# ScalarE's reads behind the latest written exponential, two buffers for the key halves, and a decoder in place, in the attention stage of a fused attention and feed-forward kernel

## The chip, the cores and the metric

One core of a Trainium2 chip runs the whole program. Its engines are TensorE (PE, and PEld for its weight loads), VectorE (DVE), ScalarE (ACT), GpSimd (POOL) and SyncE (SP, which issues nearly all DMAs). The metric is the device time of one execution in microseconds; the median of several executions is compared.

## The reference

Three layers follow each other. Shapes: q, k, v are 8 x 8 x 576 x 64 (batch, head, position, width), so there are 4608 tokens of 512 features after the attention.

```python
def _attn_ref(q, k, v):
    scores = scale * np.matmul(q, k.transpose(0, 1, 3, 2))
    mask = block_i >= block_j              # blocks of 64 positions
    scores = np.where(mask, scores, -1000000000.0)
    attn = np.exp(scores - np.max(scores, axis=-1, keepdims=True))
    attn = attn / (np.sum(attn, axis=-1, keepdims=True) + 1e-09)
    return np.matmul(attn, v)
...
def _moe_ref(x, phi, w1, w2):              # 8 experts of 4 slots
    logits = x @ phi
    d = softmax of logits over the tokens;  slot_input = d.T @ x
    slot_out[e] = np.maximum(slot_input[e] @ w1[e], 0.0) @ w2[e]
    c = softmax of logits over the slots;   return c @ slot_out
...
def _moe2_ref(x, w_in, w_out):
    h = np.maximum(x @ w_in, 0.0)
    return h * h @ w_out
```

The two matrices of the last layer, w_in (512 x 2048) and w_out, arrive as 64-bit floats; the kernel turns them into 32-bit floats itself, which it calls decoding.

## The kernel before, in words

**Stages.** The attention comes first and fills the span up to about 430 us; the logits and the token softmax of the expert layer run inside it, one batch behind. Then come the experts, then the feed-forward layer.

**The attention's loop.** Two heads make a pair; there are 32 pairs, four per batch (`j` is the pair's number in its batch, `b` the batch). `pair(n)` writes in one go: the scores and exponentials of pair `n` (`scores`, seven chunks: six of 128 x 512 at line 552 and a small one, `pd`, at line 534), the maxima of pair `n + 2` (`maxpass`, seven chunks, reduced by VectorE at line 451), the product with v of pair `n - 1` (`pv`), and the preparation of pair `n + 3` (`split`). `split` has ScalarE write a 16-bit high half of q (`high_q`) and of k (`high`, line 401, into the tile `ka`), VectorE the low half next to it (`low`, line 405), and SP transposes `ka` into `s1` by DMA (line 412). The q half is turned on TensorE and copied out by ScalarE (line 425).

**Slots.** The code of a pair is laid out over eight slots. In slot `i` stand chunk `i` of the scores with its exponential, and chunk `i` of the maxima. Slot 0 also has the two last chunks of the maxima, `split`, and nearly all of `pv`. After a slot's chunks up to four loads are taken from the queue `dq`, then one step from `aux`, or if that is empty (and not in slot 0) one from `decq`, and in some slots one step from `work` (the expert layer's softmax of the batch before).

- `aux` gets, in each odd pair from the third to the 27th, `scale` for the pairs `n + 4` and `n + 5`: four squares with a running sum on ScalarE (`square`, line 342, output `junk`, one each for k and q of two pairs), then `chain`, which begins with the TensorE matmul `ps_ssq` (line 349) and goes on with eight small VectorE steps to the scales `sig` and `es`. So the squares stand in slots 0 to 3 and `ps_ssq` in slot 4. Pairs 1 and 2 hold the same for pairs 4 to 6.
- `decq` gets the steps of one w_in chunk: `flush` on ScalarE (line 168), then `keep`, `shift`, `sign`, `low` on VectorE (lines 172 to 190). There are 16 chunks of 512 KB; each is loaded by `load_in` (line 894) into one of two `raw` buffers.
- `dq` gets, in pair `n`, the loads of q and k of pair `n + 7` (lines 316, 323) and of v of pair `n + 2` (lines 294, 300), a w_in chunk when one is due, and some chunks of the experts' weights (lines 152, 154).

**Order.** The whole loop stands under

```python
        with tc.manual_schedule(engines={mybir.EngineType.PE}):
            for n in range(N + 1):
                pair(n)
```

so TensorE runs its instructions as the code writes them. On the other engines the compiler's scheduler chooses the order when the program is built: by readiness in its own model of the time, then by the place in the code. On the chip each engine then runs its list in that order, and an instruction whose operand isn't there holds all that come after it on that engine. Semaphores between the engines are put in by the compiler.

**Buffers.** PSUM: six banks `ps_r` are shared by scores, maxima and small products, and two more take `pv`. SBUF: `ka` and `qa` have one buffer each in the pool `nat` (pairs 1 and 3 borrow others); the decoder has one `dec_sq` and one `dec_hf` of 2 KB per partition in the pool `dec`; q and k of one batch lie in one of two arenas, `ar_lo` and `ar_hi`.

Of the kernel before, what the change touches and what calls it, by code (L numbers as in the profile page):

```python
# [8 lines left out]
F32 = mybir.dt.float32  # L9
F32R = mybir.dt.float32r  # L10
F16 = mybir.dt.float16
U32 = mybir.dt.uint32
# [11 lines left out]
def tile_attn_soft_moe_ffn(  # L24
# [43 lines left out]
    lg = const.tile([128, NTILE, NSL], F32, name="lg")  # L68
    acc = const.tile([128, DM], F32, name="acc")
    tot = const.tile([128, 1], F32, name="tot")  # L70
    so = const.tile([128, KD, NSL], F32, name="so")
    mrun = [const.tile([128, 1], F32, name=f"mrun{i}") for i in range(2)]

    lo_p = ctx.enter_context(tc.tile_pool(name="low", bufs=1, side="right"))
# [28 lines left out]

    wots = {}
    w_st = ExitStack()

    def qk_tile(b):
        t = (ar_lo, ar_hi[:, 9 * 512:18 * 512])[b % 2].rearrange("p (w x j d) -> p w x j d", w=2, j=NJ, d=D)
        return dict(q=t[:, 0], k=t[:, 1])
# [52 lines left out]
    def decode(pool, dst, raw, w):  # L162
        hi, lo = raw[:, :, 1], raw[:, :, 0]
        t = {}

        def flush():
            t["sq"] = pool.tile([128, w], F32, tag="dec_sq", name="dec_sq")
            nc.scalar.activation(out=t["sq"], in_=hi.bitcast(F32), func=AF.Square)

        def keep():  # L170
            t["hf"] = pool.tile([128, w], F32, tag="dec_hf", name="dec_hf")
            nc.vector.scalar_tensor_tensor(
                out=t["hf"], in0=t["sq"], scalar=2.0 ** -30, in1=hi.bitcast(F32), op0=ALU.is_ge, op1=ALU.mult
            )

        def shift():
            t["b"] = t["sq"].bitcast(U32)
            nc.vector.tensor_scalar(
                out=t["b"], in0=t["hf"].bitcast(U32), scalar1=3, scalar2=0x3FFFFFF8,
                op0=ALU.logical_shift_left, op1=ALU.bitwise_and,  # L180
            )

        def sign():
            nc.vector.scalar_tensor_tensor(
                out=t["b"], in0=t["hf"].bitcast(U32), scalar=0xC0000000, in1=t["b"],
                op0=ALU.bitwise_and, op1=ALU.bitwise_or,
            )

        def low():
            nc.vector.scalar_tensor_tensor(  # L190
                out=dst.bitcast(U32), in0=lo, scalar=29, in1=t["b"], op0=ALU.logical_shift_right, op1=ALU.bitwise_or
            )

        return [flush, keep, shift, sign, low]
# [29 lines left out]
    def attention():  # L224
# [111 lines left out]
        def scale(ns):  # L336
            w = len(ns)
            small = lambda nm, k=2, bufs=2: sm_p.tile([128, k, 2], F32, tag=nm, name=nm, bufs=bufs)[:, :, 0:w]
            ssq = sm_p.tile([128, 2, w], F32, tag=f"ssq{w}", name="ssq")

            def square(i, nm, c):
                nc.scalar.activation(
                    out=junk, in_=qk_tile(ns[c] // NJ)[nm][:, :, ns[c] % NJ, :], func=AF.Square, accum_out=ssq[:, i, c:c + 1],
                    saturate=False,
                )

            def chain():
                ps = ps_r.tile([128, 512], F32, tag="r", name="ps_ssq")
                nc.tensor.matmul(ps[:, 0:2 * w], ones[:, 0:1].to_broadcast([128, 128]), ssq.rearrange("p a c -> p (a c)"), start=True, stop=True)
                a, hb, g, inv = [small(nm) for nm in ("sc_a", "sc_h", "sc_g", "inv")]  # L350
                sig, es = small("sig", bufs=4), small("es", 1, 4)
                nc.vector.tensor_scalar(
                    out=a, in0=ps[:, 0:2 * w].rearrange("p (a c) -> p a c", a=2), scalar1=1e-30, scalar2=None, op0=ALU.max
                )
                nc.vector.tensor_scalar(
                    out=hb.bitcast(U32), in0=a.bitcast(U32), scalar1=1, scalar2=0x7F800000,
                    op0=ALU.logical_shift_right, op1=ALU.bitwise_and,
                )
                nc.vector.tensor_scalar(
                    out=g.bitcast(U32), in0=hb.bitcast(U32), scalar1=0x7F800000, scalar2=None,  # L360
                    op0=ALU.bitwise_xor,
                )
                nc.vector.tensor_scalar(out=sig, in0=g, scalar1=2.0 ** -51, scalar2=None, op0=ALU.mult)
                nc.vector.tensor_scalar(out=inv, in0=hb, scalar1=2.0 ** 50, scalar2=None, op0=ALU.mult)
                nc.vector.scalar_tensor_tensor(
                    out=sig[:, 1], in0=inv[:, 0], scalar=2.0 ** 20, in1=sig[:, 1], op0=ALU.mult, op1=ALU.min
                )
                nc.vector.scalar_tensor_tensor(
                    out=inv[:, 1], in0=sig[:, 0], scalar=2.0 ** -20, in1=inv[:, 1], op0=ALU.mult, op1=ALU.max
                )  # L370
                nc.vector.scalar_tensor_tensor(
                    out=es[:, 0], in0=inv[:, 0], scalar=1.0 / float(D) ** 0.5, in1=inv[:, 1],
                    op0=ALU.mult, op1=ALU.mult,
                )
                for c, n in enumerate(ns):
                    sc[n] = (sig[:, :, c], es[:, 0, c:c + 1])

            return [lambda i=i, nm=nm, c=c: square(i, nm, c) for c in range(w) for i, nm in ((1, "k"), (0, "q"))] + [chain]
# [3 lines left out]
        def split(n):  # L382
            b, j = divmod(n, NJ)
            if n in (1, 3):
                qa, ka = [
                    xT_p.tile([128, S], F32, tag="xt", name=nm).bitcast(F16).rearrange("p (s a d) -> p s a d", a=2, d=D)
                    for nm in ("qa", "ka")
                ]
                qa = qa[:, :, 0, :]
            else:  # L390
                qa = nat_p.tile([128, NBLK, D], F16, tag="qa", name="qa")
                ka = nat_p.tile([128, NBLK, 2, D], F16, tag="ka", name="ka")
            tr = (tr_a, tr_a, even, odd)[j]
            t1 = tr.tile([128, NBLK, 128], F16, tag="t1", name="t1")
            s1 = tr.tile([128, NBLK, 128], F16, tag="s1", name="s1")
            qbn, s2n = qb[n % NBQ], s2[n % NB2]
            T[n] = [t1, s1, None, s2n]
            r = qk_tile(b)

            def high(nm, i, hi):  # L400
                nc.scalar.activation(out=hi, in_=r[nm][:, :, j, :], func=AF.Copy, scale=sc[n][0][:, i:i + 1])

            def low(nm, i, hi, lo):
                x = r[nm][:, :, j, :]
                nc.vector.scalar_tensor_tensor(
                    out=lo, in0=x, scalar=sc[n][0][:, i:i + 1], in1=hi, op0=ALU.mult, op1=ALU.subtract
                )

            def prep_k():
                high("k", 1, ka[:, :, 0, :])  # L410
                low("k", 1, ka[:, :, 0, :], ka[:, :, 1, :])
                nc.sync.dma_start_transpose(out=s1, in_=ka.rearrange("p s a d -> p (s a d)"))

            high_q = lambda: high("q", 0, qa)
            low_q = lambda: low("q", 0, qa, qbn[:, :, 0:D])

            def turn_q(s0, s1_):
                ps = ps_r.tile([128, 512], F32, tag="r", name="ps_qT").bitcast(F16)
                for s in range(s0, s1_):
                    for h in range(2):  # L420
                        nc.tensor.transpose(
                            ps[64 * h:64 * h + 64, 128 * (s - s0):128 * (s - s0) + 128], qa[:, s, :], id16,
                            tile_position=(0, 64 * h),
                        )
                nc.scalar.copy(t1[:, s0:s1_, :].rearrange("p s c -> p (s c)"), ps[:, 0:128 * (s1_ - s0)])

            return [high_q, lambda: [turn_q(0, 8), turn_q(8, NBLK)], prep_k, low_q]
# [77 lines left out]
        def scores(n):  # L505
# [22 lines left out]
            def chunk(i):  # L528
                ps = ps_r.tile([128, 512], F32, tag="r", name="ps_sc")
                if i == 6:  # L530
                    for kk, qq, second in ((s1, t1, False), (s2t, t2, True)):
                        nc.tensor.matmul(ps[:, 0:128], kk[:, 8, :], qq[:, 8, :], start=not second, stop=second)
                    pt = pd_p.tile([128, 2, 64], F32, tag="pd", name="pd")
                    nc.scalar.activation(
                        out=pt, in_=ps[:, 0:128].rearrange("p (h c) -> p h c", h=2), func=AF.Exp, scale=es[:, 0:1]
                    )
                    P[n]["d"] = pt
                    return
                hp, c = divmod(i, 3)
# [9 lines left out]
                    one(ps, hp, 3, 320, 3, False)  # L549
                    tail(ps, hp, 3, 448, True)  # L550
                pt = p_p.tile([128, 512], F32, tag="p", name="p")
                nc.scalar.activation(out=pt, in_=ps, func=AF.Exp, scale=es[:, 0:1])  # L552
                P[n][hp, c] = pt
                if c == 2:
                    a_, b_, c_ = P[n][hp, 0], P[n][hp, 1], P[n][hp, 2]
# [495 lines left out]
    def experts():  # L1051
# [11 lines left out]
        ep = st.enter_context(tc.tile_pool(name="ep", bufs=1))  # L1063
        cts["cs_p"] = ep
        si = ep.tile([128, KD, 2 * NSL - SPE], F32, name="si")
        nc.gpsimd.memset(si, 0.0)
        ps = ps_w.tile([128, 512], F32, tag="dx", name="ps_si")
        for dt in range(KD):
# [515 lines left out]
```

## Time and profile before

| | us |
|---|---|
| median of 3 runs | 916.43 (916.15 to 917.5) |
| the profiled execution | 917.05 |
| its span, first to last instruction | 915.2 |
| TensorE busy (matmuls) | 835.4, 91% of the span |
| VectorE busy | 685.7, 75% |
| ScalarE busy | 628.3, 69% |
| GpSimd busy | 235.0, 26% |
| granted TensorE clock, mean | 0.966 of full speed |

The busy times are unions of the instructions' own durations; waiting for a semaphore isn't in them. The shares are means over stages with different limits. The granted clock is 1.0 at 2.4 GHz and 0.5 at 1.2 GHz.

### The profile page before, as it was taken

The page shows a single profiled execution, that of the slowest core. Times are in us where ns is not written, and L with a number is a line of the kernel's source. Part 1 is how long each engine was busy: PE and PEld are TensorE (multiplying, and loading weights), DVE is VectorE, ACT ScalarE, POOL GpSimd, SP SyncE. Part 2 cuts the span into 40 slices and gives each one's busy share as a digit, 9 for nine tenths or more (in the row PEclk, how much of TensorE's full clock was granted, in tenths as well). Part 3 has the DMA queues.
Part 4 walks back from the last instruction along what each step waited for, and adds up shares of the span by engine and source line. Part 5 has one row for each costly group of instructions (what it writes and reads, how often), then busy time and mean ns, then how long its engine had stood idle before and what let it go on. Part 6 is the DMA issues. An engine that isn't in the chain of part 4 may idle for free.

```text
span 915.2 us, 22002 instructions
## 1 busy us (share of the span) xinstructions
PE 835.4 (91%) x8788; PEld 618.0 (68%) x8788; DVE 685.7 (75%) x1600; ACT 628.3 (69%) x1012; POOL 235.0 (26%) x394
## 2 busy tenths in 40 slices
PE   2778998898989889998997799989999999999997
PEld 2445766566666666766623344768988899988897
DVE  5767797888959789874641777998888778888881
ACT  5588776676748676654312688878877788888770
POOL 0234645546454465755200000000000000000000
PEclk9789999999979999999999799989999999999999
DMA  8797797989879988788999700100000100000002
GB/s 165 151 163 153 158 195 167 174 163 177 164 135 177 166 170 181 129 165 237 331 338 359 297 0 1 47 24 25 24 25 24 43 27 24 25 24 24 25 24 47
DMA packets 225191, 113.18 MB, mean 124 GB/s; under 512 B 193856, under 2 KB 202048, under 8 KB 225088
## 3 DMA queue, kind: packets, MB, share of 16 engines
q1 hardware_dynamic: 222432, 111.12, 52.5%
q8 instruction: 69, 1.13, 0.5%
q10 hardware_dynamic: 2656, 0.66, 0.4%
q14 instruction: 34, 0.28, 0.1%
HBM read 78.71 MB, written 9.44 MB: 96 GB/s over the span
## 4 chain that ended last, share of the span: by engine, by line
PE 64%; DVE 12%; DMA 11%; ACT 5%; SPq 4%; issue 3%; POOL 1%; ACTq 0%; DVEq 0%
PE ps_y L1419 14%; PE ps_z L1419 9%; PE ps_x L1419 9%; PE xm L587 5%; PE ps_sc L514 4%; PE po L1447 4%; PE ps_hb L1392 3%; DVE pm L451 2%; PE ps_max L437 2%; PE ps_u L688 2%; PE ps_h L1138 2%; DMA raw<-in_moe_w_in_dram 2%; DMA ar_lo<-in_k_dram 2%; DMA ar_hi<-in_moe_w_out_dram 1%; DMA s<-s 1%
## 5 line engine op out<-in xcount | busy, mean ns | idle before, releaser
L1419 PEld LDWEIGHTS <-ah 128*128 128x128 f16 x1792 | 171.5, 98 | 26.6 <-issue 4.0
L552 ACT ACTIVATE p<-ps_sc,es 128x512 f32<-128x512 f32 x192 | 127.9, 694 | 40.9 <-PE ps_sc L523 24.3
L1365 DVE TENSOR_TENSOR al<-a,ah 128x1024 f16<-128x1024 f32 (+1 forms) x128 | 139.4, 1126 | 19.7 <-ACT ah L1410 18.2
L451 DVE TENSOR_REDUCE pm<-ps_max 128x4 f32<-128x512 f32 x160 | 107.7, 684 | 41.7 <-PE ps_max L445 41.2
L557 POOL TENSOR_TENSOR ss<-p 128x384 f32<-128x384 f32 (+1 forms) x128 | 84.3, 679 | 197.9 <-ACT p L552 197.7
L1410 ACT CAST ah<-a 128x1024 f16<-128x1024 f32 (+1 forms) x128 | 114.7, 937 | 21.9 <-DVE a L1365 20.6
L514 PE MATMUL ps_sc<-t,s 128*128 128x512 f16 (+3 forms) x512 | 108.9, 307 | 14.8 <-ACT p L552 6.3
L1531 POOL TENSOR_TENSOR ot<-u,p 128x256 f32<-128x256 f32 x16 | 13.7, 855 | 381.9 <-DVE u L1497 366.1
L1419 PE MATMUL ps_y<-bh,ah 128*128 128x256 f16 x384 | 105.9, 276 | 3.6 <-DVE u L1497 3.6
L1419 PE MATMUL ps_y<-bh,al 128*128 128x256 f16 x384 | 105.8, 276 | 0.0
L1419 PE MATMUL ps_y<-bl,ah 128*128 128x256 f16 x384 | 105.8, 276 | 0.0
L557 POOL TENSOR_TENSOR ss<-ss,p 128x320 f32<-128x320 f32 (+1 forms) x128 | 96.6, 755 | 14.6 <-ACT p L552 6.1
L1419 PEld LDWEIGHTS <-al 128*128 128x128 f16 x896 | 88.1, 98 | 10.9 <-DVE al L1365 0.4
L1303 ACT ACTIVATE r<-ps_hb,alpha 128x1024 f32<-128x1024 f32 x64 | 71.2, 1112 | 30.8 <-PE ps_hb L1392 30.2
L587 PE MATMUL xm<-p,ar_hi 128*64 128x256 f32 (+3 forms) x512 | 90.8, 454 | 0.0
L1365 DVE TENSOR_TENSOR a<-a 128x256 f32<-128x256 f32 x192 | 75.6, 422 | 3.6
L437 PE MATMUL ps_max<-s,t 128*128 128x128 f16 (+3 forms) x256 | 63.3, 313 | 8.5 <-ACT p L552 5.0
L1419 PE MATMUL ps_x<-bh,ah 128*128 128x256 f16 x256 | 70.2, 274 | 0.2 <-ACT s L1500 0.2
L1304 ACT ACTIVATE a<-r 128x1024 f32<-128x1024 f32 x64 | 67.6, 1056 | 3.7 <-DVE al L1365 2.7
L1419 PE MATMUL ps_x<-bh,al 128*128 128x256 f16 x256 | 69.9, 273 | 0.2 <-DVE al L1365 0.2
L1419 PE MATMUL ps_z<-bh,ah 128*128 128x256 f16 x256 | 69.9, 273 | 0.0
L1419 PE MATMUL ps_x<-bl,ah 128*128 128x256 f16 x256 | 69.9, 273 | 0.0
(255 smaller groups left out, 1847.8 us busy)
## 6 DMA issues: line engine op xcount, KB each, us to landing
wch<-in_moe_w_dram SPq DMA_DIRECT2D x12, 1024.0 KB, 9.3
ar_hi<-in_v_dram SPq DMA_DIRECT2D x64, 128.0 KB, 3.1
raw<-in_moe_w_in_dram SPq DMA_DIRECT2D x16, 512.0 KB, 5.1
wch<-in_moe_w_dram SPq DMA_DIRECT2D x16, 512.0 KB, 9.6
out_dram<-ot SPq DMA_DIRECT2D x32, 256.0 KB, 2.2
ar_hi<-in_moe_w_dram SPq DMA_DIRECT2D x6, 1024.0 KB, 7.3
s<-s SPq DMA_DIRECT2D x32, 144.0 KB, 3.3
ar_lo<-in_k_dram SPq DMA_DIRECT2D x32, 128.0 KB, 4.0
```

Source lines behind the costliest of these rows:

```text
L437: nc.tensor.matmul(ps[:, c0:c0 + 128 * (u + 1)].rearrange("p (s c) -> p s c", c=128), t1[:, 2 * u + hp, :], s1[:, hp:2 * u + 2:2, :], star ...
L451: nc.vector.tensor_reduce(out=o, in_=i, axis=AX.X, op=ALU.max)
L514: nc.tensor.matmul(ps[:, c0:c0 + w].rearrange("p (s c) -> p s c", c=128), kk[:, 2 * t + hp, :], qq[:, 2 * u0 + hp:8:2, :], start=(c0 == 0 ...
L552: nc.scalar.activation(out=pt, in_=ps, func=AF.Exp, scale=es[:, 0:1])
L557: add = lambda o, x, y: nc.gpsimd.tensor_tensor(out=o, in0=x, in1=y, op=ALU.add)
L587: nc.tensor.matmul(box["xm"][64 * hp:64 * hp + 64, 128 * t:512], vs[:, t, hp, :], r, start=(t == 0), stop=(t == 3),)
L1303: nc.scalar.activation(out=r[:, c0:c1], in_=ps[:, c0:c1], func=AF.Relu, **kw)
L1304: nc.scalar.activation(out=o, in_=r[:, c0:c1], func=AF.Square)
L1365: sub = lambda o, a, b: nc.vector.tensor_tensor(out=o, in0=a, in1=b, op=ALU.subtract)
L1410: cast = nc.scalar.copy(v(H[:, kk]), v(x))
L1419: nc.tensor.matmul(acc[:, 0:HM], a[:, k], b[:, k], start=bool(first and k + j == 0), stop=(k == KH - 1 and j == 2), skip_group_check=not f ...
L1447: nc.tensor.matmul(pos[t], g[:, 512 * a + 128 * t:512 * a + 128 * t + 128], tt[:, c, a], start=(c == 0 and a == 0), stop=(c == KH - 1 and ...
```

## The change

Five edits, all but the last in the attention stage. (1) A list `exps` holds the exponential of the scores that the code wrote last. `after_exp(x)` gives a ScalarE instruction `x` a dependency on it; the dependency orders the two in ScalarE's list and has no semaphore. (2) It is applied to the decoder's `flush`, to each `square`, and to the high half of k. The high half of q has none. What is written before the first exponential isn't touched. (3) `ka` has two buffers. (4) The decoder's `keep` writes into the destination in `tin`, and `shift` and `sign` read it there; the buffer `dec_hf` is gone. (5) The tile `so` of the expert stage moves from the pool of constants to that stage's own pool.

```diff
@@ constants @@
-    so = const.tile([128, KD, NSL], F32, name="so")
...
+    exps = []
+
+    def after_exp(x):
+        if exps:
+            tc.add_manual_dep(
+                x.ins, exps[-1].ins.name,
+                mybir.DependencyInfo(mybir.DependencyClass.NoSync, mybir.DependencyReason.DATA), reason="order",
+            )
...
@@ decode @@
-            nc.scalar.activation(out=t["sq"], in_=hi.bitcast(F32), func=AF.Square)
+            after_exp(nc.scalar.activation(out=t["sq"], in_=hi.bitcast(F32), func=AF.Square))
...
-            t["hf"] = pool.tile([128, w], F32, tag="dec_hf", name="dec_hf")
             nc.vector.scalar_tensor_tensor(
-                out=t["hf"], in0=t["sq"], scalar=2.0 ** -30, in1=hi.bitcast(F32), op0=ALU.is_ge, op1=ALU.mult
+                out=dst, in0=t["sq"], scalar=2.0 ** -30, in1=hi.bitcast(F32), op0=ALU.is_ge, op1=ALU.mult
             )
...
-                out=t["b"], in0=t["hf"].bitcast(U32), scalar1=3, scalar2=0x3FFFFFF8,
+                out=t["b"], in0=dst.bitcast(U32), scalar1=3, scalar2=0x3FFFFFF8,
...
-                out=t["b"], in0=t["hf"].bitcast(U32), scalar=0xC0000000, in1=t["b"],
+                out=t["b"], in0=dst.bitcast(U32), scalar=0xC0000000, in1=t["b"],
...
@@ scale: square @@
-                nc.scalar.activation(
-                    out=junk, in_=qk_tile(ns[c] // NJ)[nm][:, :, ns[c] % NJ, :], func=AF.Square, accum_out=ssq[:, i, c:c + 1],
-                    saturate=False,
-                )
+                after_exp(nc.scalar.activation(
+                    out=junk, in_=qk_tile(ns[c] // NJ)[nm][:, :, ns[c] % NJ, :],
+                    func=AF.Square, accum_out=ssq[:, i, c:c + 1], saturate=False,
+                ))
...
@@ split @@
-                ka = nat_p.tile([128, NBLK, 2, D], F16, tag="ka", name="ka")
+                ka = nat_p.tile([128, NBLK, 2, D], F16, tag="ka", name="ka", bufs=2)
...
-                nc.scalar.activation(out=hi, in_=r[nm][:, :, j, :], func=AF.Copy, scale=sc[n][0][:, i:i + 1])
+                x = nc.scalar.activation(out=hi, in_=r[nm][:, :, j, :], func=AF.Copy, scale=sc[n][0][:, i:i + 1])
+                if nm == "k":
+                    after_exp(x)
...
@@ scores: the small chunk, and the same at the large ones @@
-                    nc.scalar.activation(
+                    exps[:] = [nc.scalar.activation(
                         out=pt, in_=ps[:, 0:128].rearrange("p (h c) -> p h c", h=2), func=AF.Exp, scale=es[:, 0:1]
-                    )
+                    )]
...
-                nc.scalar.activation(out=pt, in_=ps, func=AF.Exp, scale=es[:, 0:1])
+                exps[:] = [nc.scalar.activation(out=pt, in_=ps, func=AF.Exp, scale=es[:, 0:1])]
...
@@ experts @@
+        so = ep.tile([128, KD, NSL], F32, name="so")
```

## Rows read from the trace of the kernel before

**Rows 1.** windows: busy time and count of each engine, granted clock, DMA share, GB/s

```profile
60.00:420.00 360.00, 330.51 (x4516) 233.38 (x4514) 289.62 (x778) 250.81 (x514) 195.15 (x335) 0.97 0.88 170
```

**Rows 2.** TensorE's waits, 60 to 420 us: total us, times, longest

```profile
PE ps_sc L514 <- ACT p L552: 6.3, 4, 2.2
...
PE ps_sc L514 <- DMA s<-s: 3.3, 2, 1.8
...
PE ps_max L437 <- DVE qb L490: 0.6, 1, 0.6
...
PE ps_sT L651 <- ACT p L552: 0.4, 1, 0.4
```

**Rows 3.** ScalarE's waits, 60 to 420 us

```profile
ACT dec_sq L168 <- DMA raw<-in_moe_w_in_dram: 16.7, 9, 4.1
...
ACT ka L401 <- DMA s<-ka: 9.0, 6, 2.4
...
ACT junk L342 <- DMA ar_hi<-in_k_dram: 7.3, 4, 2.9
...
ACT junk L342 <- DMA ar_lo<-in_k_dram: 5.1, 3, 3.8
```

**Rows 4.** timeline, TensorE and ScalarE, pair 17: start, us, instruction, idle before it

```profile
255.24 1.06 PE L688 MATMUL ps_u<-phi,xt 128*128 128x64 f32 x8
...
255.27 0.71 ACT L552 ACTIVATE p<-ps_sc,es 128x512 f32<-128x512 f32 x1
...
259.41 0.36 PE L349 MATMUL ps_ssq<-ssq,ones 128*128 128x4 f32 x2
...
261.58 0.66 ACT L168 ACTIVATE dec_sq<-raw 128x512 f32<-128x512 f32 x1 [4.06 <-DMA raw<-in_moe_w_in_dram]
...
262.15 1.25 ACT L552 ACTIVATE p<-ps_sc,es 128x512 f32<-128x512 f32 x2
...
262.87 1.97 PE L688 MATMUL ps_u<-phi,xt 128*128 128x64 f32 x8 [3.09 <-ACT p L552]
```

**Rows 5.** ScalarE's groups by line, 0 to 227.2 us

```profile
L552 ACT ACTIVATE p<-ps_sc,es 128x512 f32<-128x512 f32 x90 | 59.3, 692 | 13.8 <-PE ps_sc L514 8.5 <-PE ps_sc L523 5.1
```

**Rows 6.** timeline, SP, ScalarE and TensorE, end of pair 14

```profile
219.75 1.19 SPq L316 DMA_DIRECT2D ar_hi<-in_k_dram  x2
...
224.55 0.68 ACT L342 ACTIVATE junk<-ar_hi 128x576 fp8e4<-128x576 f32 x1 [1.39 <-DMA ar_hi<-in_k_dram]
...
225.96 0.66 PE L792 MATMUL ps_x<-ident,xt 128*128 128x128 f32 x4 [1.91 <-ACT p L552]
```

**Rows 7.** windows by pair: 5 to 23, then 15, 13 and 17

```profile
93.04:348.07 255.03, 232.35 (x3125) 164.03 (x3123) 207.43 (x561) 181.49 (x377) 136.05 (x237) 0.96 0.89 168
...
227.29:239.17 11.88, 11.88 (x171) 8.08 (x170) 11.23 (x36) 9.46 (x23) 6.70 (x10) 1.00 0.83 169
...
199.63:214.28 14.65, 13.64 (x175) 11.07 (x172) 10.07 (x30) 8.35 (x19) 9.40 (x19) 0.90 0.77 165
...
251.19:269.66 18.47, 15.38 (x175) 12.79 (x172) 9.34 (x29) 9.81 (x22) 10.48 (x21) 0.81 0.72 145
```

**Rows 8.** the tile raw: time from its load's issue to landing

```profile
DMA to landing us min/median/max: 4.3/5.1/5.7
```

**Rows 9.** timeline, ScalarE and TensorE, pair 15

```profile
232.44 0.71 ACT L552 ACTIVATE p<-ps_sc,es 128x512 f32<-128x512 f32 x1
...
234.28 0.30 ACT L775 ACTIVATE d<-d 128x128 f32<-128x128 f32 x1
...
235.73 0.36 PE L349 MATMUL ps_ssq<-ssq,ones 128*128 128x4 f32 x2
...
236.35 0.67 ACT L342 ACTIVATE junk<-ar_hi 128x576 fp8e4<-128x576 f32 x1
```

**Rows 10.** SP's waits, 60 to 420 us

```profile
SPq L498 <- DVE qb L493: 11.6, 8, 3.1
```

**Rows 11.** the page: head

```profile
span 915.2 us, 22002 instructions
```

## The prediction

> **What bounds the kernel now.** First the table of stages: from 60 to 420 us the attention stage runs with TensorE busy 330.5 of 360 us at a granted clock of 0.97 [rows 1]. If TensorE is the engine that the others serve there, the stage can lose at most two things: the 29.5 us in which TensorE stands, and the half-rate time behind the 0.03 that is missing from the clock, 0.03 x 360 = 10.8 us of work. So I read next who TensorE waits for. Nine rows of its waits name an exponential (p) or a transposed copy (t) of ScalarE, from 6.3 down to 0.4 us; they add up to 22.8 us. The waits for DVE and for the copies s<-s are four rows more, 3.3 us down to 0.6, together 6.2 [rows 2]. Then, what ScalarE waits for: 16.7 us for w_in chunks (nine of sixteen flushes), 9.0 us for the transpose that still reads the only ka buffer, 12.4 us for landing k tiles in front of squares [rows 3]. ScalarE works its queue in order, so an exponential behind such a wait is late although its scores are done. One place shows it whole: the flush at 261.58 stood 4.06 us for its chunk, two exponentials follow it at once at 262.15, TensorE's logits waited 3.09 us for them, and the same eight matmuls that took 1.06 us before took 1.97 us after, since the clock had fallen to half [rows 4].
>
> The reader should also see why ScalarE stands there. Fifteen times six large exponentials lie before 227.2 us, so pair 14 ends and pair 15 begins there [rows 5]. In pair 14 SP issues a k load at 219.75, and at 224.55 a square has waited 1.39 us for a k tile [rows 6]. The code loads pair n+7 in pair n, which is pair 21 here, and writes its squares three pairs later, in pair 17. The scheduler moved that square ahead by some 20 exponentials, up to the edge of its load. The flush at 261.58 is the tenth; following the queues by hand, it is written in pair 20 and ran in pair 17.
>
> By pairs: the 19 from 93.04 to 348.07 (5 to 23) take 13.42 us each with the clock at 0.96; pair 15, in which TensorE met no stall, takes 11.88, and pairs 13 and 17, each with a wait for a chunk in it, take 14.65 and 18.47 [rows 7]. In pair 15 TensorE never stands, and DVE is busy 11.23 of 11.88: a second engine is close.
>
> **The change, part by part.**
>
> *Order on ScalarE.* No instruction is added; 101 reads (56 squares, 29 k halves, 16 flushes) must now follow the exponential written last before them. Both sides are on ScalarE, so this costs no semaphore. What it removes: the squares then stand three pairs behind their load and the flushes more than one, so 12 us or more against the 4.3 to 5.7 us that a w_in chunk takes to land [rows 8]. So I take the waits of [rows 3] as gone, and TensorE's 22.8 us with them. Bounds: 0 (another wait stands right behind each) and 22.8.
>
> *The second ka buffer* removes the six waits for s<-ka (in the 22.8 already). The held k half would do most of that alone, since it now runs once per pair. A k half of an even pair comes four to five exponentials later; then its transposes leave one pair ahead of the first matmul that needs them, as those of odd pairs do already, and no row of TensorE's waits names s<-ka. Cost nothing; the cover is that lead, and a transpose later by more than it would hold TensorE up directly.
>
> *Decoder in place.* keep writes the tin tile instead of dec_hf, the two steps after it read tin: the same instructions on the same shapes. Nothing. *so in the expert stage's pool*: the same tile at another address, used only after the attention. Nothing. Both pay for the ka buffer's space.
>
> *Clock.* The 10.8 us come back where no long idle is left. Some falls will stay, since short idles remain; between 0 and 10.8 I take 7.
>
> *The new wait.* TensorE's order is written by hand and does not move: the matmul ps_ssq of a pair stands in slot 4 of every odd pair from 3 to 27, behind four squares (slots 0 to 3). Before, these squares were done long ahead. Now the fourth may not start before the exponential of slot 3. In pair 15 the exponential of slot 1 starts at 232.44 and ps_ssq at 235.73. A square holds ScalarE 0.67 us (the row at 236.35), an exponential 0.57 (two of them 1.25 long, overlapping [rows 4]), so three of each are 3.7 us, plus 0.3 for the small exponentials of the running softmax at 234.28: the fourth square ends about 236.5, and TensorE stands 0.8 us [rows 9]. Pair 17 has 4.1 us between the same two points (255.27, 259.41) [rows 4]: there the wait is about nil. Five pairs like 15 give 4 us, eight others 0 to 0.5 each; I take 6, with bounds 0 and 13 x 0.8 = 10. Queued behind a waiting ps_ssq are the scores of slots 5 and 6, and behind those the next pair.
>
> *The next limiter.* DVE and copy waits of 6.2 us exist [rows 2]; with the stage 20 us shorter DVE is busy 290 of 340 us [rows 1]. I add 4, bounds 0 and 6.2.
>
> *Moved loads.* A w_in chunk is loaded into one of two buffers, and the decoder now frees them later, so SP issues these loads later. SP stands often enough to take that: its largest wait, for DVE ahead of the transpose t<-qb, is 11.6 us in eight times [rows 10]. Cost 0; were it not so, the k and transposed tiles queued behind a blocked chunk would come late.
>
> *Sum:* -22.8 - 7 + 6 + 4 = -19.8 us. Start-up (before 60 us) and what follows 420 us I leave alone: the expert stage's loads start when the attention frees their room, so it shifts with it. The profiled execution took 917.05 us, 915.2 of it span [rows 11]; 917.05 - 19.8 = 897.25, and the median of the runs, 916.43, lies 0.6 below the profiled one: **896.6 us**.
>
> **The rivals.**
>
> *A, the gain is mostly eaten* by ps_ssq and DVE. For it: DVE at 11.23 of 11.88 in a pair without stalls, ScalarE at 9.46 [rows 7]. Against: pair 15 carried almost that load with TensorE never idle. With the upper bounds and no clock back: -22.8 + 10 + 6.2 = -6.6, so 905 to 914.
>
> *B, the chunk loads slip with the flushes.* Two raw buffers: load i+2 waits for decode i, which is now late, so the flush meets its load in flight again. For it: only two buffers. Against: from the end of one decode to the flush two further on lie some eight exponentials or more, over 12 us, against 5.7 [rows 8]. Then only the squares' and ka's share stays, (9.0 + 12.4) of 38.1 = 56% of 22.8 + 7, and the same +10: -7, or 909.
>
> *C, the loads set the pace*, and ScalarE's waits only show it. For it: DMA share 0.88 over the stage [rows 1]. Against: at a share of 1 the same bytes would need 360 x 0.88 = 317 us, 43 less than now, and SP waits for DVE [rows 10]. It would give 916.4, no change. The Trainium skill (Perfetto Trace Analysis, What "DMA-bound" means) counts a kernel as DMA-bound also where the issuing engine's track is solid with DMA slices; by that rule the time would stay at 916.4. The trace does not agree: SP's waits for DVE are gaps in that track.
>
> *D, slower.* Place: ps_ssq in the 13 odd pairs. If each wait were 1.5 us and brought a fall of the clock like pair 13's, which cost 0.10 x 14.65 = 1.5 us [rows 7], that is 13 x 3.0 = 39 us against 33.6 at most removed: +5, 922. It decides from 33.6 / 13 = 2.6 us per odd pair. For it: in pair 13 TensorE stood 1.0 us in all (13.64 of 14.65 busy), and the clock was 0.90 all the same. Against: pair 15 ran at 1.00 right after an idle of 1.91 that ended at 225.96 [rows 6], and my wait is 0.8. The Trainium skill (TensorE: Matmul & The Clock Gate, A second HAM failure mode: psum-queue depth-cycling) says that brief but frequent idles between groups of matmuls make the clock swing between its levels, 1.2 and 2.4 GHz; by that rule D's condition is met. The trace agrees for some idles and not for others.
>
> **How the numbers follow.** Chances: the forecast (884 to 905) 0.53; A 0.22; B 0.06; better than all bounds, by start-up gains, 0.04; C 0.06; D 0.09. The low end is the full bound, 33.6 us off; the high end takes in A and B and most of what is between: 884 to 914. The repeats spread by 0.15%, so I call 0.2% (1.8 us) the edge of no change: faster 0.85, same 0.06, slower 0.09.
>
> **What would show it.** In the profile after: ScalarE's waits for in_moe_w_in, in_k and s<-ka near zero; pair 17 near 12.5 us; 60:420's work done some 20 us earlier with the clock nearer 1.00; new rows "ps_ssq <- junk" of under 1 us each, thirteen at most. Wrong would be: chunk waits still there (B), ps_ssq waits over 1.5 us or a clock below 0.97 (D), SP rows that wait for the decoder, or the same span with TensorE now waiting for transposes (s<-ka, t<-qb) or DVE.

## The result, and the profile after

The changed kernel took 903.32 us, the median of four runs (902.38 to 905.82), against 916.38 us (916.15 to 917.5) for the kernel before beside it: a ratio of 0.9859, 95% interval 0.9838 to 0.9881, so 13.1 us faster. The forecast was 896.6, in a range of 884 to 914: the way was right, and two thirds of the size came. The profiled execution is the slowest of the four, 905.82 us, so its span lies only 11.2 us below that of the profile before.

The head and the busy times of the page after:

```profile
span 904.0 us, 22000 instructions
...
PE 831.6 (92%) x8788; PEld 615.2 (68%) x8788; DVE 693.3 (77%) x1600; ACT 627.1 (69%) x1012; POOL 248.7 (28%) x394
```

Next, what ScalarE waits for in the kernel after, 60 to 420 us (total us, times, longest), the view that answers to [rows 3]; its four largest rows:

```profile
ACT xt L642 <- PE xm L595: 47.1, 24, 5.4
ACT p L560 <- PE ps_sc L531: 18.8, 28, 1.6
ACT p L560 <- PE ps_sc L522: 12.0, 15, 6.0
ACT al L769 <- DVE nm L768: 10.2, 5, 2.0
```

No row names a w_in chunk, a k tile or a load of ka any more: the 38.1 us of [rows 3] are gone, and ScalarE now stands mostly for results of TensorE. The view of the tile raw shows the flushes' room: the loads land in 5.1 us at the median as before (7.7 at most, 5.7 before), and the first flush runs at 137.0 us instead of 117.0.

```profile
L175 ACT ACTIVATE dec_sq<-raw x16: 654/682/707, 137.0 to 373.8; 128x512 f32<-128x512 f32 x16
...
DMA to landing us min/median/max: 4.5/5.1/7.7
```

TensorE's waits in the same stretch answer to [rows 2]; the five largest rows:

```profile
PE ps_ssq L355 <- ACT junk L348: 7.1, 7, 1.3
PE ps_sc L522 <- DMA s<-s: 5.5, 3, 5.1
PE ps_sT L659 <- ACT qa L407: 4.3, 5, 0.9
PE ps_max L445 <- DMA s<-ka: 3.7, 5, 1.5
PE ps_max L445 <- DVE pm L459: 1.0, 1, 1.0
```

All nine rows on ScalarE's exponentials and copies t are gone. In their place stand the square in front of ps_ssq, which was forecast, and two rows that were not, for the q half (qa) and for the transposed keys (s<-ka); the row of the copies s<-s, 3.3 us before, has grown to 5.5.

The windows after: the whole stage, then pairs 5 to 23, pairs 15 and 17 alone, and the last two stretches, pairs 24 to 27 and 28 to 30 (columns as in [rows 1]; a pair is counted from the start of its first large exponential):

```profile
60.00:420.00 360.00, 335.04 (x4648) 235.60 (x4645) 299.98 (x787) 258.19 (x534) 215.20 (x344) 0.99 0.87 173
91.14:328.45 237.31, 223.56 (x3119) 158.45 (x3120) 210.85 (x550) 178.71 (x374) 148.89 (x237) 1.00 0.91 177
216.11:229.94 13.83, 12.47 (x172) 8.29 (x170) 12.94 (x40) 10.53 (x26) 8.39 (x12) 1.00 0.97 188
239.65:253.57 13.92, 13.88 (x185) 10.78 (x185) 12.82 (x37) 10.99 (x24) 10.97 (x21) 1.00 0.83 183
328.45:378.06 49.61, 46.86 (x655) 32.94 (x653) 45.58 (x114) 36.81 (x75) 30.44 (x49) 1.00 0.76 154
378.06:420.59 42.53, 36.66 (x466) 25.30 (x465) 24.02 (x65) 18.44 (x36) 22.06 (x41) 0.92 0.76 184
```

And the last two stretches, the same pairs, in the kernel before:

```profile
348.07:393.12 45.05, 44.48 (x646) 32.27 (x643) 41.04 (x111) 31.36 (x61) 28.90 (x48) 1.00 0.75 146
393.12:430.39 37.27, 34.33 (x466) 24.04 (x465) 22.03 (x59) 17.80 (x36) 22.13 (x41) 1.00 0.88 211
```

Read as an account: before pair 5 the kernel gains 1.9 us (93.04 to 91.14). Pairs 5 to 23 gain 17.7 (255.03 [rows 7] to 237.31), half of it idle time of TensorE (22.7 to 13.75) and half busy time (232.35 to 223.56), which goes with the clock's rise from 0.96 to 1.00. So pair 24 starts 19.6 us earlier, close to the 19.8 of the forecast. Then it is given back: 4.6 us in pairs 24 to 27 and 5.3 in pairs 28 to 30. What follows 420.59 takes 483.4 us, against 484.8 after 430.39 before. Sum: 1.9 + 17.7 - 4.6 - 5.3 + 1.4 = 11.1, the 11.2 between the two spans.

The 5.3 us have a place. Timeline of the kernel after, SP and TensorE, pairs 29 and 30 (start, us, instruction, idle before it):

```profile
388.52 4.90 SPq L506 DMA_TRANSPOSE t<-qb  x1
...
393.51 1.95 SPq L161 DMA_DIRECT2D wch<-in_moe_w_dram  x2
...
395.52 1.52 SPq L918 DMA_DIRECT2D s<-s  x1
...
405.95 0.61 PE L522 MATMUL ps_sc<-t,s 128*128 128x512 f16 x1 [5.09 <-DMA s<-s]
```

And SP at the same place in the kernel before:

```profile
403.55 1.54 SPq L498 DMA_TRANSPOSE t<-qb  x1
...
407.99 1.49 SPq L910 DMA_DIRECT2D s<-s  x1
```

The copy s<-s is the second-half copy of pair 30's transposed keys, 144 KB, issued in pair 29 behind two weight chunks of 1 MB. It landed 10.4 us after its issue, and TensorE stood 5.09 us for it; the clock of that stretch is 0.92. Of the 5.3 us, 2.9 are idle time of TensorE and 2.3 busy time. Before, the same copy went out at 407.99, also behind weights, took 10.3 us, and TensorE stood 1.5. Counted from the start of pair 29 (402.83 before, 387.80 after), the copy goes out 2.6 us later than before (5.2 to 7.7), and TensorE needs it 0.9 us sooner (14.0 to 13.1). SP shows where most of that arises: the transpose t<-qb in front of the copy starts at the same place, 0.7 us into the pair, and holds SP for 4.90 us instead of 1.54.

The 4.6 us of pairs 24 to 27 look different. Groups of ScalarE in these four pairs, first in the kernel before:

```profile
L168 ACT ACTIVATE dec_sq<-raw 128x512 f32<-128x512 f32 x1 | 0.7, 673 | 0.0
```

and in the kernel after:

```profile
L348 ACT ACTIVATE junk<-ar_hi 128x576 fp8e4<-128x576 f32 x6 | 4.2, 697 | 0.0
...
L175 ACT ACTIVATE dec_sq<-raw 128x512 f32<-128x512 f32 x4 | 2.7, 679 | 0.0
```

Before, the squares and all flushes but one had run ahead into earlier pairs, and these four were light: 11.26 us each. Now they carry their own share and take 12.40, close to the 12.49 of pairs 5 to 23. But 1.4 of the 4.6 us are only where the stretch begins: before, the first exponential of pair 24 started 2.04 us behind the first matmul of its scores (346.03), because ScalarE first wrote a k half, and after only 0.63 us behind it (327.82). Windows from that matmul to the same one of pair 28, before and after, hold the same 655 records of TensorE:

```profile
346.03:392.49 46.46, 45.89 (x655) 32.83 (x653) 42.45 (x115) 32.27 (x62) 29.58 (x49) 1.00 0.74 146
327.82:377.43 49.61, 46.86 (x655) 32.94 (x653) 45.54 (x116) 36.98 (x76) 30.44 (x49) 1.00 0.76 155
```

So the pairs themselves are 3.1 us longer: TensorE's named waits grew by 1.9 (0.6 to 2.5), its busy time by 1.0. VectorE's busy time in them grew by 3.1 as well (42.45 to 45.54): 13 steps of the decoder, 10.3 us, fall in these pairs, against 8 steps, 6.4 us, before.

### The profile page after: what moved, and what is told of

The parts are those of the page before. It is cut to its first block, busy times and chain, and to the rows that moved or that the text cites. A ratio compares the mean times of both kernels' runs of the same rounds, so it can differ in the third digit from the quotient of the medians.

```text
span 904.0 us, 22000 instructions
## 1 busy us (share of the span) xinstructions
PE 831.6 (92%) x8788; PEld 615.2 (68%) x8788; DVE 693.3 (77%) x1600; ACT 627.1 (69%) x1012; POOL 248.7 (28%) x394
## 4 chain that ended last, share of the span: by engine, by line
PE 66%; DVE 14%; DMA 10%; ACT 5%; SPq 3%; issue 2%; ACTq 0%; DVEq 0%
PE ps_y L1428 14%; PE ps_z L1428 9%; PE ps_x L1428 9%; PE xm L595 5%; PE po L1456 4%; PE ps_sc L522 4%; DMA s<-ka 3%; PE ps_hb L1401 3%; DVE pm L459 2%; PE ps_u L696 2%; PE ps_max L445 2%; PE ps_h L1147 2%; DMA s<-s 1%; PE tl L606 1%; DMA raw<-in_moe_w_in_dram 1%
## 5 line engine op out<-in xcount | busy, mean ns | idle before, releaser
L560 ACT ACTIVATE p<-ps_sc,es 128x512 f32<-128x512 f32 x192 | 129.1, 695 | 45.7 <-PE ps_sc L531 21.9
L1374 DVE TENSOR_TENSOR al<-a,ah 128x1024 f16<-128x1024 f32 (+1 forms) x128 | 139.5, 1128 | 19.8 <-ACT ah L1419 18.3
L565 POOL TENSOR_TENSOR ss<-p 128x384 f32<-128x384 f32 (+1 forms) x128 | 90.8, 730 | 179.1 <-ACT p L560 178.8
L565 POOL TENSOR_TENSOR ss<-ss,p 128x320 f32<-128x320 f32 (+1 forms) x128 | 101.0, 789 | 11.5 <-ACT p L560 2.8
L1428 PE MATMUL ps_z<-bl,ah 128*128 128x256 f16 x256 | 69.8, 273 | 0.0
```

The source lines that it names most:

```text
L560: exps[:] = [nc.scalar.activation(out=pt, in_=ps, func=AF.Exp, scale=es[:, 0:1])]
L565: add = lambda o, x, y: nc.gpsimd.tensor_tensor(out=o, in0=x, in1=y, op=ALU.add)
L1374: sub = lambda o, a, b: nc.vector.tensor_tensor(out=o, in0=a, in1=b, op=ALU.subtract)
L1428: nc.tensor.matmul(acc[:, 0:HM], a[:, k], b[:, k], start=bool(first and k + j == 0), stop=(k == KH - 1 and j == 2), skip_group_check=not f ...
```

## The experiments

The edits are against the changed kernel. All ratios are to the kernel before on the same chip, whose medians were 916.68 to 917.36 there; there most of its runs lay between 908.75 and 922.66. The intervals reach 3 to 6 us to either side, so a smaller difference between two experiments is not clear of noise.

**1. No order, buffer kept.** The hold is left out; the second ka buffer and the decoder in place stay.

```
-        if exps:
+        if False:
```

> The changed kernel without any held read (second ka buffer, decoder in place and the moved tile stay). Theory: the held order removes the landing waits, and the second ka buffer by itself removes only the 9 us that ScalarE waited for s<-ka; the chunk and k-tile waits (29 us on ScalarE) are back. Time 907 to 912. Rival 1, the buffer alone is the change: 902 to 905, and no landing waits. Rival 2, the buffer is worth nothing without the order: 915 to 918.

Measured: 917.44 us, ratio 1.0005 (0.997 to 1.004). The profile of it, ScalarE's waits, 60 to 420 us:

```profile
ACT dec_sq L175 <- DMA raw<-in_moe_w_in_dram: 14.9, 6, 4.2
ACT junk L348 <- DMA ar_lo<-in_k_dram: 11.4, 4, 4.7
ACT junk L348 <- DMA ar_hi<-in_k_dram: 8.6, 6, 3.3
```

The time is that of rival 2, not the 907 to 912 expected. The waits for ka are gone, as the buffer promises, and the others have grown: 34.9 us, against 29.1 without ka's 9.0 before [rows 3]. So the wait taken away gave nothing back here. Without the order the buffer, the decoder in place and the moved tile bring nothing; the gain needs the order.

**2. One ka buffer, order kept.**

```
-                ka = nat_p.tile([128, NBLK, 2, D], F16, tag="ka", name="ka", bufs=2)
+                ka = nat_p.tile([128, NBLK, 2, D], F16, tag="ka", name="ka")
```

> The changed kernel with one ka buffer again. Theory: with the k half held, each write of ka comes a pair after the last, so the buffer is free anyway: same as the changed kernel, 901.5 to 905, and no row of ScalarE that waits for s<-ka over 1 us. Rival, the second buffer carries part of the gain: 907 or more, with waits for s<-ka of several us.

Measured: 901.19 us, ratio 0.9835 (0.9779 to 0.9892), as the changed kernel within the intervals. ScalarE waited once for s<-ka, 0.4 us. The second buffer does nothing once the k half is held. The decoder in place and the moved tile stood in every run with the order; what the order does without them was not run.

**3. The copy s<-s earlier in the last pairs.** In pairs 29 and 30 (counted from 0) the copy for the next pair is put at the head of the load queue in slot 0 and not in slot 2.

```
-                if i == 2 and n + 1 < N:
+                if i == (2 if n < N - 3 else 0) and n + 1 < N:
                     dq.insert(0, lambda: s2copy(n + 1))
```

> In the last three pairs the copy s<-s of the next pair is written in slot 0 instead of slot 2, so SP issues it ahead of the experts' weight chunks. Theory: TensorE's 5.1 us in front of pair 30 come from that copy queued behind 2 MB of weights; they go, and with them the half-rate stretch that follows: 895 to 899. Rival, the weights only hit the next transfer (the transpose t<-qb) or end later and hold the experts: 902 to 905, with the wait under another name.

Measured: 897.91 us, ratio 0.9795 (0.9736 to 0.9854), 5.4 us below the changed kernel. Its pairs 28 to 30, its timeline on SP, and what is left of the wait:

```profile
375.87:411.16 35.29, 34.30 (x466) 24.30 (x465) 24.01 (x65) 18.43 (x37) 22.01 (x41) 1.00 0.89 222
```

```profile
384.86 0.49 SPq L918 DMA_DIRECT2D s<-s  x1
...
388.51 3.12 SPq L161 DMA_DIRECT2D wch<-in_moe_w_dram  x2
```

```profile
PE ps_sc L522 <- DMA s<-s: 0.3, 1, 0.3
```

The copy now goes out ahead of the two weight chunks and of t<-qb, which holds SP for 1.50 us (at 386.27). The wait in the stage is 0.3 us, and pairs 28 to 30 take 35.29 us at a clock of 1.00, against 42.53, and 37.27 in the kernel before. That the 5.3 us given back there come from this copy and its place in SP's queue is shown.

**4. The matmul ps_ssq one slot later.** In the pairs whose row sums cover two pairs, an empty step stands between the squares and the chain that begins with ps_ssq.

```
-            return [lambda i=i, ...] + [chain]
+            return [lambda i=i, ...] + [lambda: None] * (w == 2) + [chain]
```

> The chain with ps_ssq stands one slot later (slot 5) in the odd pairs. Theory: TensorE's waits for the fourth square (7.1 us in seven rows from 60 to 420 us) fall under 1 us and the time with them: 896 to 900. Rival, ScalarE's load in those slots is the limit and not the place of ps_ssq, or the scales then come late for the q halves: waits move to ps_qT, ps_sT or ps_sc and the time stays at 902 to 905.

Measured: 899.37 us, ratio 0.9812 (0.9744 to 0.988). TensorE's waits:

```profile
PE ps_sT L659 <- ACT p L560: 5.5, 5, 1.1
PE ps_ssq L355 <- ACT junk L348: 3.5, 7, 0.9
```

The wait of 7.1 us halves, where under 1 us was expected, and a row of 5.5 at ps_sT stands where 4.3 stood. All named waits of TensorE together go from 23.1 to 20.1 us; the rest moved.

**5 to 7. One kind of read held at a time.** Squares alone; flushes alone; k halves alone. The other two kinds run free. For the first, for instance:

```
-            after_exp(nc.scalar.activation(out=t["sq"], in_=hi.bitcast(F32), func=AF.Square))
+            nc.scalar.activation(out=t["sq"], in_=hi.bitcast(F32), func=AF.Square)
...
-                if nm == "k":
+                if False:
                     after_exp(x)
```

> Only the squares are held; flushes and k halves are free again. Theory: a read that is free is moved up to its landing edge, so the flushes' chunk waits (14.9 us on ScalarE without any order) stay and the k-tile waits go: 906 to 911. Rival, the squares are what matters and the scheduler has nothing early left to move: 902 to 905.

> Only the decoder's flushes are held. Theory: the chunk waits go, the squares' k-tile waits (some 20 us on ScalarE without any order) stay: 907 to 912. Rival, the chunk waits were the larger part and the time comes near the changed kernel's: 902 to 905.

> Only the high halves of k are held (with two ka buffers). Theory: both kinds of landing waits stay, and only the wait for s<-ka is gone, which the free order with two buffers did not turn into time either: 914 to 919. Rival, the k half is the read that lets the others run early: 910 or less.

Measured: squares 918.63 us, ratio 1.0025 (0.9993 to 1.0057); flushes 916.02, 0.9984 (0.9952 to 1.0016); k halves 916.87, 0.9996 (0.9957 to 1.0036). None gains. ScalarE's waits, with the squares held:

```profile
ACT dec_sq L175 <- DMA raw<-in_moe_w_in_dram: 23.3, 8, 5.0
```

and with the flushes held:

```profile
ACT junk L348 <- DMA ar_lo<-in_k_dram: 10.6, 6, 4.6
...
ACT junk L348 <- DMA ar_hi<-in_k_dram: 9.7, 6, 2.9
```

The right comparison is experiment 1, which has the same buffers and holds nothing: 14.9 us for chunks, 20.0 for k tiles. With the squares held, the chunk waits grow to 23.3. With the flushes held, the k-tile waits stay at 20.3, so ScalarE's landing waits fall from 34.9 to 20.3 us, and yet the time does not fall. The windows of that run show where it went, pairs 5 to 23 and 28 to 30:

```profile
96.77:341.10 244.33, 225.48 (x3119) 162.44 (x3118) 209.16 (x551) 179.34 (x374) 150.37 (x237) 0.98 0.86 170
...
390.39:433.00 42.61, 35.68 (x466) 24.58 (x465) 23.54 (x63) 17.79 (x35) 21.33 (x40) 0.92 0.76 184
```

Pairs 5 to 23 take 11.3 us less than in experiment 1 (255.67). But pairs 24 to 27 take 4.3 more than there (49.29 against 44.95) and pairs 28 to 30 take 5.5 more (37.10 there), with a wait of 6.2 us for a copy s<-s. So the held flushes do gain in the middle, and the end of the stage takes it. With the squares alone or the k halves alone the middle does not gain that (259.64 and 253.57 us). The flushes alone with experiment 3's copy were not run. The expectation that each part brings its share was wrong for the first two.

**8. The hold let go from pair 20 on,** to see whether the flushes that come late are what makes pairs 24 to 27 long.

```
-        if exps:
+        if exps and cur[0] < 20:
```

> The changed kernel, but reads written in pair 20 or later are not held. Theory: the changed kernel's pairs 24 to 27 take 49.6 us against 45.1 before, because reads and decoder steps that ran ahead before now fall there; released, they run early again, those pairs shrink by 3 to 5 us, and landing waits come back in pairs 19 to 23, up to as much: 901 to 905. Rival, those pairs are slow for another cause (weights on the DMA queues): they stay at 49 to 50 us.

Measured: 908.02 us, ratio 0.9896 (0.9858 to 0.9934), 4.7 us above the changed kernel (the intervals overlap). Pairs 24 to 27 took 50.60 us, no less than 49.61. One w_in chunk is waited for again (1.8 us), and TensorE stands for DVE and for s<-ka (3.1 us once, 5.9 in five). Two flushes still ran in these pairs, against four in the changed kernel and one before. So this miss does not decide the cause: only half of what came late was taken out, and letting the reads go also let other waits in.

**9. Experiments 3 and 4 together.**

> Both the earlier copy s<-s in the last three pairs and the chain one slot later. Theory: the copy's stall and the ps_ssq waits are separate places, so the two gains add: about 4 to 6 us from the one and 3 to 4 from the other, 893 to 896. Rival, one hides the other: 897 to 899.

Measured: 894.29 us, ratio 0.9769 (0.9728 to 0.981). 897.91 and 899.37 are 5.4 and 3.95 below the changed kernel, together 9.4; measured 9.0. The sum fits two separate waits, within intervals of 4 to 6 us.

**10. Squares and flushes held, k halves free.** Only the second part of the diff of experiment 5.

> Squares and flushes are held, the high halves of k are free (two ka buffers). Theory: the three kinds do not add, because whatever landing read is left free is moved up and stalls instead; the k half does not read a fresh load, its operand landed long ago, so leaving it free costs little: 901 to 906. Rival, the k half must be held too (it then waits for its scales, and with it the exponentials): 910 or more.

Measured: 900.99 us, ratio 0.9844 (0.9794 to 0.9895), all of the gain. TensorE's waits:

```profile
PE ps_ssq L355 <- ACT junk L348: 7.1, 7, 1.3
...
PE ps_sT L659 <- ACT p L560: 6.8, 5, 1.4
...
PE ps_max L445 <- DMA s<-ka: 1.5, 1, 1.5
```

No landing wait is left on ScalarE. Neither of the two holds shortens the run alone and both together bring everything; the third is not needed where ka has two buffers.

**11. Experiment 9, and the q halves held too.**

```
-                if nm == "k":
-                    after_exp(x)
+                after_exp(x)
```

> As the kernel with the earlier copy and the later chain, and the high half of q held like that of k. Theory: the waits of ScalarE for the qa buffer (qa <- DVE qb, 6 to 7 us) go and with them TensorE's at ps_sT, a gain of 1 to 4 us on that kernel. Rival, the q half then comes too late for its turn on TensorE in the same slot (ps_qT waits for qa): 2 to 10 us slower than that kernel.

Measured: 890.94 us, ratio 0.9732 (0.9686 to 0.9777), the fastest of all: 26 us below the kernel before on its chip. TensorE's waits and the stage:

```profile
PE ps_x L799 <- DVE pm L458: 3.5, 5, 0.7
PE ps_ssq L355 <- ACT junk L348: 3.4, 7, 0.9
```

```profile
60.00:420.00 360.00, 345.85 (x4861) 244.43 (x4857) 303.16 (x806) 265.95 (x547) 220.37 (x352) 1.00 0.92 186
```

That is 3.4 us below experiment 9, with intervals that overlap. The row at ps_sT is gone, and the largest is now ps_x, where TensorE stands 3.5 us for VectorE's maxima pm. In the changed kernel the q half did not wait for a DMA but for VectorE's step qb, which reads the only buffer qa (7.0 us in five times); held, it has no such row any more.

**12. Held behind the last exponential but one,** with experiment 3's copy: a milder hold, instead of the later ps_ssq.

```
-                x.ins, exps[-1].ins.name,
+                x.ins, exps[0].ins.name,
...
-                exps[:] = [nc.scalar.activation(out=pt, in_=ps, func=AF.Exp, scale=es[:, 0:1])]
+                exps[:] = exps[-1:] + [nc.scalar.activation(out=pt, in_=ps, func=AF.Exp, scale=es[:, 0:1])]
```

> The earlier copy, and each read held behind the last exponential but one instead of the last. Theory: the fourth square is done a slot earlier, so the ps_ssq waits (7.1 us) fall under 2, with no landing waits yet since the loads are still a pair or more behind: 892 to 895. Rival, ScalarE is full in these slots either way and the wait moves to ps_sT or ps_sc: 896 to 899.

Measured: 894.52 us, ratio 0.9771 (0.9731 to 0.9811), level with experiment 9. TensorE's waits:

```profile
PE ps_sT L659 <- ACT qa L407: 5.9, 5, 1.2
...
PE ps_ssq L355 <- ACT junk L348: 2.7, 5, 0.7
```

The wait at ps_ssq goes from 7.1 us to 2.7, not under the 2 expected; that at ps_sT grows from 4.3 to 5.9, and the copies s<-s cost 4.6 us in three waits.

## Why the prediction was right, and where its size was off

**The waits removed: right.** The landing waits are gone, and with them TensorE's 22.8 us. Experiments 1 and 2 show that the order does it: without it the time is that of before, and without the second buffer the gain stays. The tenth flush, which ran in pair 17, now runs in pair 20, as the prediction had followed it by hand. Pair 17, which waited for a chunk, takes 13.92 us instead of 18.47 [rows 7]; forecast was near 12.5, and its TensorE idle is nil (13.88 busy). Pair 15, which had no stall, lost: 11.88 to 13.83, with the new wait in it and 40 DVE instructions instead of 36. The work is spread more evenly, so a pair without stalls was too good a mark for all pairs; the mean is 12.49.

**The clock: right.** I took 7 us of at most 10.8. By the same reckoning the stage's 0.99 leaves 0.01 x 360 = 3.6, so 7.2 came back. Pairs 5 to 23 alone got 8.8 us of busy time back, at 1.00; pairs 28 to 30 lost some of it again at 0.92.

**The new wait at ps_ssq: right.** 6 us were forecast, in up to 13 rows of under 1 us; it is 7.1 in seven rows, the longest 1.3. Timeline of the kernel after, pair 15:

```profile
225.16 0.67 ACT L560 ACTIVATE p<-ps_sc,es 128x512 f32<-128x512 f32 x1
225.73 0.67 ACT L348 ACTIVATE junk<-ar_hi 128x576 fp8e4<-128x576 f32 x1
226.30 0.19 ACT L348 ACTIVATION_READ_ACCUMULATOR junk<-ar_hi 128x1 f32 x1
...
226.54 0.38 PE L355 MATMUL ps_ssq<-ssq,ones 128*128 128x4 f32 x2 [1.16 <-ACT junk L348]
```

It is the mechanism that the prediction told, the last square behind the exponential of its slot; 1.16 us here against 0.8 worked out, which did not count the reads of the accumulator behind the squares (0.19 us each). Rival D needed 2.6 us per odd pair and a falling clock. The Trainium skill (TensorE: Matmul & The Clock Gate, A second HAM failure mode: psum-queue depth-cycling) has frequent brief idles between groups of matmuls swing the clock. The trace shows no swing from these: seven of them in the stage, and 1.00 over pairs 5 to 23.

**The second ka buffer "cost nothing": half right.** It costs nothing because it does nothing (experiment 2). But the held k half does make its transposes late: s<-ka holds TensorE five times, 3.7 us, which I had put at nothing. With the k halves free (experiment 10) that row is 1.5 us, and ps_sT stands 6.8 behind exponentials, so it moves.

**The moved loads: nearly nothing, as forecast.** SP waits for the decoder in front of a chunk's load twice, 2.6 us in all (L902 <- DVE tin), which the prediction had named as a sign of being wrong. No wait for a chunk came of it; whether it made the s<-ka rows is not shown.

**The next limiter: the term that was mis-sized.** I took 4 us with 6.2 as the bound, from the waits that already had a row. The waits that took over (ps_sT for the q half, s<-ka, the copies s<-s, DVE's x and pm) come to 16.0 us after, against 6.2 of the same kind before [rows 2], so 9.8 more. With the measured terms the prediction's sum is -22.8 - 7.2 + 7.1 + 9.8 = -13.1 us, so this term holds nearly all of what the forecast was short. A bound that is read from the rows of before holds only for waits that were not hidden behind the one removed.

**Where it fell: at the end of the stage.** What the prediction left alone behind 420 us did only shift (483.4 us behind pair 30, against 484.8). But it counted the end of the attention as if it were like the middle. By pair 24 all 19.6 us were there; pairs 24 to 30 then gave 9.8 back. Of it, 5.3 us belong to the copy of pair 30: it is timed by SP's queue, with weights and a long transpose in front, and it did not come earlier by as much as TensorE did. Experiment 3 shows it. Of the other 4.6, 1.4 are where the stretch begins and 3.1 are longer pairs. That goes with the held flushes: from matmul to matmul the four pairs take 48.6 to 49.6 us in the nine profiles with the flushes held throughout (the changed kernel, experiments 2 to 4, 6 and 9 to 12), and 45.7 to 47.4 in the four with them free (the kernel before, experiments 1, 5 and 7). That the cause is work that ran ahead before and now falls due, so that part of the gain in the middle was work pushed back and not time won, fits VectorE's steps counted above. Experiment 8, which took half of these flushes out, did not shorten the pairs. It is argued and not shown.

**The rivals.** A was the nearest: its price, 905 to 914, begins 1.7 us above the result, and what was missing from the forecast went mostly to transfers and the q half, which it did not name; ps_ssq, which it named, took 1.1 us more than forecast. B did not happen: no wait for a chunk is left. C is refuted: the same loads run in 13 us less, and in 26 less in experiment 11. Why experiment 1 came out as it did I had not foreseen either: the gains of the parts do not add up. One part of the reason shows with the squares: with them alone held, the free flushes stall more (14.9 to 23.3 us). For the flushes it is another: held alone they gain, and the end of the stage takes it. The low end of the prediction's range would be 882.8 by its own numbers (916.4 - 33.6), not 884; nothing hangs on it.

## What to carry to other kernels

Where a scheduler writes the order of an in-order engine, hold all reads that it moves to the edge of a landing, not only the worst kind: here one kind alone left the time where it was (918.6, 916.0 and 916.9 us), and two kinds gave everything (901.0). Before dropping a part that gave nothing, read its time by stretches: the held flushes gained 11.3 us in the middle, and the end of the stage hid it. Then walk through the end of the shortened stage: what is issued by another engine's queue need not come earlier by as much, and a small transfer that the next step needs belongs in front of the large ones (5.4 us here for one copy).

## What was not expected of the hardware

A copy of 144 KB usually landed 3.1 us after its issue (the median of 32) and took 10.4 us when issued right behind two loads of 1 MB; one transpose t<-qb held SP for 4.90 us behind two more weight chunks, and 1.54 before and 1.50 in experiment 3, each behind one.

The clock stood at 1.00 over pairs 5 to 23 although TensorE stood for ps_ssq (seven times in the stage, 1.0 us in the mean). After the idle of 5.09 us at 405.95 the windows give 0.55 for the next 6 us, so the wait for that copy cost more than its own length:

```profile
405.95:412.00 6.05, 6.05 (x49) 3.13 (x53) 0.00 (x0) 1.06 (x2) 0.00 (x0) 0.55 0.73 231
```

The time of the kernels with the flushes, the squares or both free spread widely: 914.62 to 925.56 us over ten runs with only the squares held, 911.05 to 919.6 with only the flushes. With both held it spread less: 900.77 to 902.87 over four runs in experiment 10, 887.96 to 893.33 over six in experiment 11. These have fewer runs, and four runs of the kernel before lay within 1.4 us too. That the spread comes from the landings is argued from this, and was not measured by itself.
